# Attention in four 64x64 tiles, two sequences loaded head by head, and its vector and scalar work dealt out over the slots behind each burst

## The chip, the cores and the metric

The kernel runs on one core of one Trainium2 chip. The metric is the device time of one execution in microseconds (us), the median over several executions; lower is better. The profile is of one execution. Its span is some 1.8 us shorter than the device time of the same run (217.5 against 219.34 for the kernel before). The engines are TensorE (PE in the profile, and PEld for its weight loads), VectorE (DVE), ScalarE (ACT), GpSimd (POOL) and SyncE (SP). L and a number is the source line that issued an instruction, and the numbers differ from kernel to kernel.

## The reference

Retention with a decay per head, then a feed-forward layer with the snake activation. It is cut to what matters.

```python
# q, k, v: (4 sequences, 8 heads, 768 tokens, 64)
gamma = 1.0 - 2.0 ** (-5.0 - np.arange(H))
for t in range(S):
    state = gamma * state + outer(k[:, :, t], v[:, :, t])     # 64 x 64 per head
    y[:, :, t] = scale * einsum('bhd,bhde->bhe', q[:, :, t], state)
x = y.transpose(0, 2, 1, 3).reshape(3072, 512)
h = x @ w_in                                                  # 512 -> 2048
g = h + sin(alpha * h) ** 2 / (alpha + 1e-9)
out = g @ w_out                                               # 2048 -> 512
```

## The kernel before

The 768 tokens of a sequence are six chunks of 128. `order` puts the first chunks of the four sequences (e0 to e3) in front, then the others sequence by sequence; P[14] is the first of the others of sequence 2. The 24 chunks form groups of 4, 2, 4, 4, 4, 4 and 2 for the feed-forward layer (the MLP). In "phase g", TensorE alternates between slots of the first matmul of group g and pieces of the second matmul of group g - 1; the attention for group g + 1 is put between them in short bursts.

A burst has four parts: the scores q·k, the mixing of the masked scores with v, the part from earlier chunks (q times the state), and the sums k·v that go into the state.

```python
    def scale_v(j, eng):                       # decay of v inside a chunk
        eng.tensor_mul(raw["v", j], raw["v", j], kg[:, j % NCH, :, None].to_broadcast([128, H, D]))
    ...                                        # cut: GpSimd does it between the loads, early

    def stage_S(j):                            # sums: the state stays in PSUM for the whole sequence
        c = j % NCH
        if c == 0:
            st["ps"] = psum.tile([128, NP, D], F32, name="ps", tag="ps")
        ps = st["ps"]
        for p in range(NP):
            for e in range(2):
                nc.tensor.matmul(ps[64 * e:64 * e + 64, p, :], raw["k", j][:, 2 * p + e, :], raw["v", j][:, 2 * p + e, :],
                                 start=(c == 0 and p == 0), stop=True, skip_group_check=True)
        return ps

    def keep_S(j, ps):                         # ScalarE casts it straight from PSUM
        for e in range(2):
            r = slice(64 * e, 64 * e + 64)
            nc.scalar.copy(s_bd[(j % NCH + 1) % 2][r, :, r], ps[r, :, :])

    def stage_M(j):
        ...                                    # cut: inter and mixing matmuls into py (one bank, tag "ty")
        ps = stage_S(j) if c < NCH - 1 else None
        nc.vector.tensor_mul(x, py, qg[:, c])  # xT, the input of the MLP
        if ps is not None:
            keep_S(j, ps)

    def phase(g, outs, att, nf=1):
        no, done = len(outs), 0
        for n in range(FF // nf):
            now = Slot(g, n * nf, nf=nf).sq("A")   # first matmul, Sin and Square on ScalarE
            for fn in att.get(n, ()):
                fn()                               # attention of this slot, if any
            now.add()                              # VectorE: gT = h + sin^2 / alpha
            while done < no * (n + 1) * nf // FF:
                outs[done]()                       # a piece of the second matmul
                done += 1
```

PSUM has eight banks here: four rotating ones ("mm"), two for the scores ("pa"), one for py ("ty") and one for the state ("ps").

## Time and profile before

| | before |
|---|---|
| time, median (range) | 219.22 us (219.15 to 219.43) |
| span of the profiled run | 217.5 us, full clock |
| busy share: TensorE, ScalarE, VectorE, GpSimd | 94%, 75%, 59%, 41% |
| stores of the state for the next chunk | 40 ScalarE casts from PSUM, 0.36 us each |
| scalings of v | 21 on GpSimd (1.06 us each), 3 on VectorE (0.74 us) |

TensorE is busy nearly all the time, so an engine beside it may be idle or late without cost as long as TensorE never waits for it. The prediction below shows the lines that say so. The columns are start (us), duration (us), engine, source line, operation, output and inputs, shapes, count, and in brackets the wait ahead of it.

### The profile page before, as it was taken

Reading aid. Unit: us, or ns where it says so; the run is one execution under the profiler, and the core shown is the slowest. Engines: PE = TensorE matmul, PEld = TensorE weight load, DVE = VectorE, ACT = ScalarE, POOL = GpSimd, SP = SyncE. Lnnn points to the kernel's source line nnn. Section 1 sums busy time; section 2 is a strip of 40 time slices with the busy share of each in tenths; the row PEclk is TensorE's granted clock in tenths of the full one; section 3 lists DMA queues with packets and bytes.
Section 4 is the critical chain, followed back from the end, with each engine's and each line's share of the span. In section 5 each row is a group of like instructions: output and inputs, shape, how many; then the busy total and the mean of one; then the engine's idle time right before and its main releaser. Section 6 shows DMA issues by size and latency. Waiting matters only on the chain.

```text
span 217.5 us, 4218 instructions
## 1 busy us (share of the span) xinstructions
PE 203.8 (94%) x1634; PEld 107.5 (49%) x1661; DVE 128.1 (59%) x213; ACT 162.8 (75%) x311; POOL 90.1 (41%) x105
## 2 busy tenths in 40 slices
PE   7798899999989999999999999999999999999992
PEld 3444554467764545445455445454544544555540
DVE  4686659867895767766466566366464555233310
ACT  7678796658889999789768768777868876766610
POOL 8975335999889885896981000000000000000000
PEclk9999999999999999999999999999999999999999
DMA  9999999999999999999999146237011101111121
GB/s 132 151 193 191 205 207 164 154 207 161 164 151 182 163 120 154 112 160 175 135 188 107 23 96 77 60 60 96 7 47 51 48 0 51 48 48 48 51 94 50
DMA packets 99508, 24.67 MB, mean 113 GB/s; under 512 B 92304, under 2 KB 96416, under 8 KB 99488
## 3 DMA queue, kind: packets, MB, share of 16 engines
q0 software_dynamic: 77024, 13.37, 84.0%
q1 hardware_dynamic: 22464, 11.02, 26.4%
q8 instruction: 13, 0.21, 0.4%
q14 instruction: 7, 0.06, 0.1%
HBM read 27.27 MB, written 6.29 MB: 154 GB/s over the span
## 4 chain that ended last, share of the span: by engine, by line
PE 74%; DVE 9%; DMA 4%; POOL 4%; ACT 4%; issue 3%; POOLq 0%; ACTq 0%
PE po L304 35%; PE ph L279 31%; DMA qkr<-in_k_dram 4%; DVE gT L294 4%; PE py L247 3%; PE pa L213 2%; POOL qkr L83 2%; ACT s L282 2%; DVE aT L217 2%; PE py L251 2%; POOL vr L83 1%; DVE xT L258 1%; PE ps L227 1%; DVE s L289 1%; ACT s L287 1%
## 5 line engine op out<-in xcount | busy, mean ns | idle before, releaser
L294 DVE SCALAR_TENSOR_TENSOR gT<-s,rec_alpha,ph 128x512 bf16<-128x512 f32 (+3 forms) x120 | 74.1, 637 | 68.1 <-ACT s L287 67.5
L279 PE MATMUL ph<-xT,w_in 128*128 128x512 bf16 (+3 forms) x478 | 97.9, 336 | 1.1 <-DVE gT L294 0.6
L304 PE MATMUL po<-w_out,gT 128*128 128x512 bf16 x360 | 94.1, 379 | 3.8 <-issue 2.9
L282 ACT ACTIVATE s<-ph,alpha_sb 128x512 f32<-128x512 f32 (+3 forms) x120 | 69.6, 601 | 34.0 <-PE ph L279 33.9
L279 PEld LDWEIGHTS <-w_in 128*128 128x128 bf16 x480 | 45.5, 98 | 42.6 <-issue 2.1
L287 ACT ACTIVATE s<-s 128x512 f32<-128x512 f32 (+1 forms) x94 | 58.4, 621 | 2.6
L304 PEld LDWEIGHTS <-gT 128*128 128x128 bf16 x384 | 35.2, 98 | 38.2 <-issue 0.6
L112 POOL TENSOR_TENSOR vr<-vr,kg 128x512 bf16<-128x512 bf16 x21 | 22.0, 1056 | 12.2 <-DMA vr<-in_v_dram 12.2
L217 DVE TENSOR_TENSOR aT<-pa,mask 128x1024 bf16<-128x1024 f32 x20 | 24.4, 1220 | 0.3 <-PE pa L213 0.3
L83 POOL DMA_DIRECT2D vr<-in_v_dram x24 | 21.7, 904 | 3.0 <-DMA w_in<-in_moe_w_in_dram 1.7
L83 POOL DMA_DIRECT2D qkr<-in_q_dram x23 | 21.3, 925 | 4.0 <-DMA w_out<-in_moe_w_out_dram 1.6
L83 POOL DMA_DIRECT2D qkr<-in_k_dram x23 | 20.4, 887 | 3.8 <-DMA w_out<-in_moe_w_out_dram 3.3
L234 ACT CAST s_bd<-ps 64x256 bf16<-64x256 f32 x40 | 14.4, 360 | 2.4 <-PE ps L227 2.1
L316 ACT COPY o_sb<-po 128x512 f32<-128x512 f32 x23 | 13.1, 576 | 3.9 <-PE po L304 3.9
L258 DVE TENSOR_TENSOR xT<-py,qg 128x512 bf16<-128x512 f32 x20 | 13.7, 684 | 2.6 <-PE py L251 2.5
L328 PE MATMUL spare<-warm 128*128 128x512 bf16 x27 | 9.3, 465 | 1.4 <-DVE warm L131 1.2
L213 PEld LDWEIGHTS <-qkT 64*128 64x128 bf16 x192 | 5.4, 94 | 9.3 <-issue 7.1
L251 PE MATMUL py<-aT,vr 128*64 128x128 bf16 x192 | 9.5, 220 | 0.4 <-DVE rec_alpha L366 0.2
L213 PE MATMUL pa<-qkT 64*128 64x128 bf16 x192 | 9.5, 219 | 0.4 <-ACT qkT L186 0.2
L247 PE MATMUL py<-qkT,s_bd 128*64 128x128 bf16 x160 | 8.3, 224 | 0.7 <-DVE xT L258 0.7
L247 PEld LDWEIGHTS <-s_bd 128*64 128x64 bf16 x160 | 5.4, 109 | 4.8 <-issue 2.0
L251 PEld LDWEIGHTS <-vr 128*64 128x64 bf16 x192 | 6.9, 110 | 1.3 <-issue 1.0
(59 smaller groups left out, 68.8 us busy)
## 6 DMA issues: line engine op xcount, KB each, us to landing
out_dram<-o_sb SPq DMA_DIRECT2D x24, 256.0 KB, 2.3
vr<-in_v_dram POOLq DMA_DIRECT2D x24, 128.0 KB, 6.2
qkr<-in_q_dram POOLq DMA_DIRECT2D x23, 128.0 KB, 5.6
qkr<-in_k_dram POOLq DMA_DIRECT2D x23, 128.0 KB, 5.8
w_in<-in_moe_w_in_dram POOLq DMA_DIRECT2D x4, 512.0 KB, 11.1
w_out<-in_moe_w_out_dram POOLq DMA_DIRECT2D x4, 512.0 KB, 14.8
q<-in_q_dram SPq DMA_DIRECT2D x1, 256.0 KB, 3.4
k<-in_k_dram SPq DMA_DIRECT2D x1, 256.0 KB, 4.7
```

Of the source, the lines that this page charges most:

```text
L83: nc.gpsimd.dma_start(out=t, in_=chunk_of(src, j))
L112: eng.tensor_mul(raw["v", j], raw["v", j], kg[:, j % NCH, :, None].to_broadcast([128, H, D]))
L213: nc.tensor.matmul(pa[:, e, p, :], qkT[r, NP + p, :], qkT[r, p, :], start=(p == 0), stop=True, skip_group_check=True)
L217: nc.vector.tensor_mul(aT.rearrange("p e n t -> p (e n) t"), pa.rearrange("p e n t -> p (e n) t"), m)
L247: nc.tensor.matmul(py[r, p, :], s_bd[c % 2][:, p, r], qkT[:, p, :], start=(p == 0), stop=True, skip_group_check=True)
L251: nc.tensor.matmul(py[64 * e:64 * e + 64, p, :], vs[:, 2 * p + e, :], aT[:, e, p, :], start=(c == 0 and p == 0), stop=True, skip_group_che ...
L258: nc.vector.tensor_mul(x, py, qg[:, c])
L279: nc.tensor.matmul(self.ph[:, m, :], w_in[:, i, f * 128:(f + 1) * 128], xT[g][:, i, self.lo:self.hi], start=(m == 0 and i == 0), stop=(i = ...
L282: nc.scalar.activation(out=self.s[:, m, :], in_=self.ph[:, m, :], func=ACTF.Sin, scale=alpha_sb[:, f:f + 1])
L287: nc.scalar.activation(out=self.s, in_=self.s, func=ACTF.Square)
L294: nc.vector.scalar_tensor_tensor(gT[self.g][:, f, self.lo:self.hi], self.s[:, m, :], rec_alpha[:, f:f + 1], self.ph[:, m, :], op0=ALU.mult ...
L304: nc.tensor.matmul(po[g, ts], gT[g][:, f, ts * C:(ts + 1) * C], w_out[:, f, :], start=(f == 0), stop=(f == FF - 1))
```

## The change

The intent: use the array of TensorE as four independent 64x64 tiles, so that a burst becomes shorter; skip the triangle above the diagonal, for which two of the four sequences are loaded so that heads, not tokens, lie in the two halves of the partitions; and spread VectorE's and ScalarE's work behind a burst over the following slots, so that none of it holds up the MLP. To give four tiles separate banks, py becomes two banks, and the bank that held the state goes: the state is now kept in SBUF in float32, VectorE adds each chunk's sums to it, and ScalarE casts the result. The diff, cut to its core:

```diff
+    def wide(j):                                   # sequences 2 and 3, but for their first chunks
+        return j % NCH > 0 and j // NCH >= 2
+    def load_seq(bt):                              # one DMA per head and tensor, 640 rows each
+        ...
+        for i, src in enumerate((q, k, v)):
+            for h in range(H):
+                ...
+                nc.gpsimd.dma_start(out=o, in_=src[bt, h, C:, :].rearrange("(f i) d -> i f d", i=64))
...
+    def keep(j, py, base=256):
+        new = py[:, :, base:base + 128].rearrange("p b (m d) -> p m b d", m=2)
+        if j % NCH == 0:
+            nc.vector.tensor_copy(s_f, new)
+        else:
+            nc.vector.tensor_add(s_f, s_f, new)
+    def hand_on(j):
+        i = (j % NCH + 1) % 2
+        if not wide(j + 1):
+            nc.scalar.copy(s_n[i], s_f)
+            return
+        s = s_w[i].rearrange("p m b (y d) -> p m (b y) d", y=2)
+        nc.scalar.copy(s[half(0), :, 0:4:3], s_f[half(0)])
+        nc.scalar.copy(s[half(1), :, 1:3], s_f[half(1)])
...
+        def leave():
+            if now is not None:
+                keep(now, py)
+            nc.vector.tensor_mul(x_of(j), py[:, :, 0:256]..., qg[:, c]...)
+        return [leave, lambda: now is not None and hand_on(now)]
+
+    def burst(old, new, first=None):
+        inter(old)
+        return scores(new) + mix(old, first)       # [mask, leave, hand_on], dealt out later
...
-            now = Slot(g, n * nf, nf=nf).sq("A")
+            now = Slot(g, n * nf, nf=nf)
+            if rest and rest[0][0] == "A":
+                rest.pop(0)[1]()                   # hand_on, between Sin and Square
+            now.sq("A")
             for fn in att.get(n, ()):
-                fn()
+                more = fn()
+                if more:
+                    rest.extend(zip("DDA" if len(more) == 3 else "DA" if len(more) == 2 else "D", more))
...
             now.add()
+            if calm and rest and rest[0][0] == "D":
+                rest.pop(0)[1]()                   # one piece per slot (in phase 1 all at once)
...
+            at(a - 3, V(j))                        # scaling of v by VectorE, three slots ahead of its burst
```

Besides, the last tile of the output is computed and stored in pieces of 256, 128 and 128 columns. Also cut here: the chunk P[6] is transposed by a DMA and no longer by TensorE, a piece of w_in comes in three DMAs instead of one, and the scores of the next chunk now stand inside a burst, between its part from earlier chunks and its mixing.

## The prediction

> **What bounds the kernel now.** I read the page's shares and chain first, to see which engine sets the end; then busy time by stage, to see where other engines come near it; then the timeline of TensorE around one attention burst, which is what the change rebuilds; last GpSimd's timeline, because the order of the loads changes.
>
> ```profile
> PE 203.8 (94%) x1634; PEld 107.5 (49%) x1661; DVE 128.1 (59%) x213; ACT 162.8 (75%) x311; POOL 90.1 (41%) x105
> ...
> PE 74%; DVE 9%; DMA 4%; POOL 4%; ACT 4%; issue 3%; POOLq 0%; ACTq 0%
> ```
>
> TensorE is the bound, with 94% of the span and 74% of the chain. The rest of the chain lies almost wholly before 65 us.
>
> Busy time of each engine by stage; I cut at the phases of the MLP (start and group 0; phase 1 from 48.2; phases 2, 3, 4, 5, 6 from 65.1, 91.1, 123.6, 155.8, 185.7; then the tail). Columns: stretch, length, PE, PEld, DVE, ACT, POOL with counts, clock, DMA share, GB/s.
>
> ```profile
> 48.20:65.10 16.90, 15.64 (x222) 12.03 (x225) 14.06 (x25) 14.40 (x33) 15.42 (x18) 1.00 2.00 161
> 65.10:91.10 26.00, 25.11 (x214) 12.49 (x217) 18.49 (x25) 22.83 (x41) 21.07 (x23) 1.00 1.94 149
> 91.10:123.60 32.50, 31.87 (x262) 15.82 (x264) 18.67 (x24) 26.06 (x48) 20.71 (x23) 1.00 1.62 136
> ```
>
> In the steady phases (3 on) TensorE is full and nothing else is close. A 512-column matmul takes 0.216 us of pitch (four in 0.86 us in the chain), so phase 3 is 128 x 0.216 = 27.6 us of MLP, and the other 4.9 us are attention. In phase 1 and 2 VectorE (14.1 of 16.9) and ScalarE (22.8 of 26.0) stand nearer. The DMA engines hold about two packets each at any moment until 123 us.
>
> One burst of phase 3 on TensorE, in the timeline:
>
> ```profile
> 101.22 0.40 PE L213 MATMUL pa<-qkT 64*128 64x128 bf16 x8
> 101.55 0.41 PE L247 MATMUL py<-qkT,s_bd 128*64 128x128 bf16 x8
> 101.79 0.39 PE L251 MATMUL py<-aT,vr 128*64 128x128 bf16 x8
> 102.02 0.29 PE L227 MATMUL ps<-vr,qkr 128*64 128x64 bf16 x8
> ```
>
> Eight 128-column matmuls occupy 0.40 us from first start to last end and one lasts 0.22, so the eight starts spread over 0.18 us: three steps of some 58 ns, two matmuls to a step. Half-array tiles already run in pairs. The 64-column sums step by about 31 ns per pair (0.29 - 0.196 over three steps). From 101.22 to 101.55 are 0.33 us for four steps of 58: the remaining 0.1 us is the change of tile shape. The same 0.1 us separates a burst from the MLP on both sides. So a burst costs 0.1 + 0.23 + 0.1 + 0.25 + 0.22 + 0.12 + 0.1 = 1.12 us; the scores alone 0.43, the mixing alone 0.79.
>
> GpSimd's timeline, the loads of the last chunk of sequence 1 and the first of sequence 2:
>
> ```profile
> 63.14 0.94 POOL L83 DMA_DIRECT2D qkr<-in_q_dram  x1
> 64.07 0.88 POOL L83 DMA_DIRECT2D qkr<-in_k_dram  x1
> 64.94 0.90 POOL L83 DMA_DIRECT2D vr<-in_v_dram  x1
> 65.83 2.07 POOL L112 TENSOR_TENSOR vr<-vr,kg 128x512 bf16<-128x512 bf16 x2
> 67.82 0.94 POOL L83 DMA_DIRECT2D qkr<-in_q_dram  x1
> ```
>
> An issue of 1024 rows costs GpSimd 0.88 to 0.94 us, and a chunk with its scaling about 4 us; the page gives 0.79 for a weight load of 512 rows.
>
> **What the Trainium skill says.** "TensorEngine Tiling (Array Packing)", section Key Properties: tiles run independently, and changing the tiling mode drains the engine. The trace agrees: pairs in 58 ns, 0.1 us at each change. "TensorE: Matmul & The Clock Gate", section The mechanism (Part 3): matmuls on disjoint row and column tiles overlap, their starts some 4 ns apart. Pairs here are 4 ns apart; four at once is not shown by this trace. "VectorE: DVE Perf Modes", section Side-by-side: about 150 cycles of fixed cost, and in the plain mode, which PSUM operands leave, one element per cycle at 0.96 GHz. For the 1024-wide mask (1024 + 150)/0.96 = 1223 ns; the trace has 1220.
>
> **The change part by part.**
>
> *Bursts, sequences 2 and 3 (head by head).* Inter: 4 full-array matmuls of 128 columns, 4 x 56 = 0.22, and no change of shape ahead of it. Change 0.1. Scores: per m one group of four 128-column and one of four 64-column tiles, 2 x (56 + 31) = 0.17, as the triangle above the diagonal is left out. Mix the same, 0.17. Sums: four groups of four, 4 x 31 = 0.12. Change 0.1, plus 0.04 for the first four weight loads. Sum 0.93 us against 1.12. *Bursts of sequences 0 and 1:* change 0.1, inter 2 x 56, scores 4 x 56, change 0.1, mix 0.22, sums 0.12, change 0.1: 0.97.
>
> Before, each phase also paid separately for the first scores and the last mix. From the phases: attention before is 4.6 (phase 2), 4.9, 4.6 and 2.2 (phase 5) = 16.2 us. After: phase 2 has three bursts of 0.97 and a mixed one of about 0.92, 3.85; its first scores (0.42) move in front; phase 3 is 4 x 0.93; phase 4 the same plus 0.1 for sums of another shape; phase 5 is 0.93 + 0.6. Sum 13.3. Gain 2.9 us, all on the path, as TensorE is the bound there. Phases 0 and 1, counted the same way with one transposition by TensorE fewer (0.45): 9.1 to 8.0, gain 1.1.
>
> *VectorE.* Each chunk gains an addition of the state, 256 wide, (256 + 150)/0.96 = 0.42 us. The wide mask falls from 1.22 to (768 + 150)/0.96 = 0.96. Fourteen scalings of v, 0.74 each, come from GpSimd (two are those of e2 and e3). Phase 2 then holds 16 x 0.745 of gT, four bursts at about 2.3, six scalings and, at its head, the new masks, two clears and the mask of the first scores (about 3): 28 us of VectorE for some 24.6 of TensorE. Most of that is backlog which three free PSUM banks can carry; I charge 0.5. Phase 1 adds 0.42 per burst where TensorE already waits 0.7 us for xT in all (the list of waits): +0.6. The shared two-bank py must be evicted before the first burst: +0.6.
>
> *Start.* Three issues per w_in piece instead of one delay the loads behind by some 2.5 us of issuing, but those land after a DMA backlog of over 9 us (the chain's longest DMA step, 9.44), so hidden. The transposition of e3 goes one slot later and fills most of its 1.2 us stall: -0.7. New tables (about 1.1 us of small VectorE work) sit ahead of the mask of e2, which releases the last xT before the MLP: +0.7.
>
> *Tail.* Now: last eviction 0.42 on VectorE, then 0.37 on ScalarE, then a 256 KB store. After: 128 columns, 0.29 us, and a quarter of the bytes: -0.8.
>
> *The loads of sequence 2.* Two thirds of it, q and k of all heads (16 issues), must land before chunk P[14] can be transposed; before, one chunk was enough. P[13] reuses the buffer of e1, free after the burst of slot 6 in phase 1, near 61.5 us. P[13] takes 2.7, the 16 issues of 640 rows about 0.8 each, 12.8, and landing 5.7 (the page): about 82. The transposing DMA takes 6.0 (its median): 88. The burst that needs it is in slot 13 of phase 2: 65 + 13 x 1.29 + three bursts and slack of 0.5 = 85.2. A stall of about 2.8 us.
>
> Sum: -2.9 - 1.1 + 0.5 + 0.6 + 0.6 + 0 - 0.8 + 2.8 = -0.3 us. I don't take it whole. The slots of the transpositions and scalings are set so finely, and only two sequences are loaded this way, that the author probably saw this wait and placed the burst behind it; I halve the stall and take a quarter off the three charges of 1.7: -0.3 - 1.4 - 0.4 = -2.1, 217.1 us.
>
> **Rivals.** (1) No load stall: loads run ahead since GpSimd no longer waits for v (12.2 us of waits on the page). For it: rows per DMA shrink from 1024 to 640. Against it: issuing, not data, then sets the pace. Time 219.2 - 3.1 = 216.1, and 214.4 if the three charges of 1.7 fall away too. (2) Load stall in full or worse, with transposes slower under it (longest landing 8.9 us), and the clock dropping in the gap: 219 to 222. (3) The four tiles don't run at once, weights loading in pairs: the 64-column groups take 62 instead of 31, +0.25 per wide burst, ten bursts, so 217.1 + 2.5 = 219.6. Half-array pairs at 31 ns speak against it. (4) VectorE bounds phase 2 wholly: +3 us, but this hides the load stall, as both delay the same slots: 218.6.
>
> **Range and chances.** All four tiles, no stall and no charge give 214.4; the stall with a cold clock 220 to 221. Range 214.2 to 220.4. Faster by over 2% means under 214.9, which needs nearly every gain and no stall: 0.17. Slower by over 2% means above 223.6: 0.04. Within 2%: 0.79.
>
> **What will show it.** Wide bursts of 0.93 us between MLP matmuls (if 1.2, the tiles don't overlap). Phase 3 of 31.4 us instead of 32.5. In phase 2 a wait of TensorE on the transposed qkT of P[14], near 85 us. VectorE above 90% busy in phase 2. The end 2.8 us or less after the last eviction. The prediction is wrong if phase 3 doesn't shorten, or if a wait outside phase 2 exceeds 2 us.

## More of the kernel before

One more piece of that timeline is needed for the comparison: what happens after a burst of phase 3.

```profile
101.32 0.69 ACT L282 ACTIVATE s<-ph,alpha_sb 128x512 f32<-128x512 f32 x1 [0.38 <-PE ph L279]
...
102.05 0.63 ACT L287 ACTIVATE s<-s 128x512 f32<-128x512 f32 x1
...
102.47 0.81 PE L304 MATMUL po<-w_out,gT 128*128 128x512 bf16 x3 [0.16 <-issue]
102.58 0.73 ACT L234 CAST s_bd<-ps 64x256 bf16<-64x256 f32 x2
102.80 0.68 DVE L258 TENSOR_TENSOR xT<-py,qg 128x512 bf16<-128x512 f32 x1
```

ScalarE finishes the slot's Sin and Square first, and then casts the state, which waits for nobody but TensorE. VectorE has only the mask and the product xT to do.

## The result, and the profile after

The changed kernel takes 233.13 us (232.25 to 233.76, four runs) against 219.19 us of the kernel before in the same rounds. The ratio is 1.0635, 95% interval 1.0595 to 1.0676: 6.35% slower. The profiled run was at full clock. A ratio here is the mean time of one kernel's fast runs over that of the other's in the same rounds, so it is not quite the ratio of the medians that are quoted. Executions over 1.5% slower than the fastest of the same kernel are left out of the means.

The page's shares and chain of the changed kernel:

```profile
PE 202.1 (87%) x1921; PEld 108.3 (47%) x1949; DVE 144.1 (62%) x261; ACT 160.4 (69%) x301; POOL 86.0 (37%) x115
...
PE 48%; ACT 21%; DVE 14%; issue 9%; DMA 6%; SPq 0%; DVEq 0%; ACTq 0%
```

TensorE's busy time is even a little less than before, and no other engine is near being full. But TensorE's share of the chain that ended last fell from 74% to 48%, and ScalarE and VectorE came in with 21% and 14%. Nothing new is a bound; TensorE waits more. Busy time in the changed kernel's phases 2, 3 and 4 (the columns are as in the prediction):

```profile
72.30:103.10 30.80, 24.38 (x250) 12.03 (x254) 23.76 (x37) 21.50 (x37) 26.59 (x38) 1.00 2.06 159
103.10:136.30 33.20, 31.35 (x333) 15.65 (x337) 21.56 (x32) 25.51 (x45) 3.86 (x6) 1.00 0.60 84
136.30:170.50 34.20, 31.65 (x324) 15.75 (x328) 22.16 (x33) 25.44 (x45) 0.00 (x0) 1.00 0.30 63
```

Phase 2 takes 30.8 us instead of 26.0 and phase 3 33.2 instead of 32.5, with up to 6.4 us of TensorE idle in phase 2 against 0.9 (26.00 - 25.11) before; a few matmul records are missing in both. VectorE is busy for 77% of phase 2 (23.76 of 30.80), so it doesn't bound that phase. (Phase 1 is another matter: see e11.)

Are the bursts shorter? One burst of phase 3 on TensorE, in the timeline (the weight-load lines inside the burst are left out):

```profile
122.12 0.39 PE L347 MATMUL py<-qkT,s_w 128*128 128x128 bf16 x4
...
122.43 0.25 PE L372 MATMUL pa<-qkT 64*64 64x128 bf16 x4
...
122.51 0.20 PE L376 MATMUL pa<-qkT 64*64 64x64 bf16 x4
...
122.63 0.23 PE L394 MATMUL py<-aT,v_seq 64*64 64x128 bf16 x4
...
122.80 0.30 PE L313 MATMUL py<-v_seq,qk_seq 64*64 64x64 bf16 x16
123.03 0.55 PEld L463 LDWEIGHTS <-gT 128*128 128x128 bf16 x4
```

Yes. From the first inter matmul to the first MLP weights after the burst are 0.91 us. (The trace lacks the record of that first MLP matmul. In the complete trace of e3_both, below, the gap between MLP matmuls is 0.917 us.) The prediction's 0.93 and the four overlapping tiles hold. The time is lost beside the bursts, and the list of waits names where:

```profile
ACT s_n L328 <- DVE s_f L322: 6.3, 6, 2.2
...
PEld L390 <- DVE vr L142: 4.4, 4, 2.0
PEld L352 <- ACT s_n L328: 4.2, 4, 1.5
...
PE py L390 <- DVE vr L142: 3.5, 3, 1.9
...
PE ph L439 <- DVE xT L406: 3.3, 4, 1.4
...
PE ph L439 <- ACT o_sb L467: 2.5, 8, 1.0
```

Each line is the waiting engine, what it waited for, us in all, times, and the longest. Of these the list of the kernel before has only TensorE's waits for the cast state (1.3 us) and for an eviction (0.2 us). Now ScalarE waits 6.3 us for VectorE's addition of the state, TensorE waits for the cast state (s_n), for scaled v (vr), for the product xT and for ScalarE's eviction of an output tile (o_sb). Two of these are worth reading closely. First, what follows a burst of phase 3, in the timeline:

```profile
126.70 0.69 ACT L442 ACTIVATE s<-ph,alpha_sb 128x512 f32<-128x512 f32 x1 [0.38 <-PE ph L439]
127.02 0.41 DVE L322 TENSOR_TENSOR s_f<-s_f,py 128x256 f32<-128x256 f32 x1
...
127.47 0.40 ACT L331 CAST s_w<-s_f 64x256 bf16<-64x256 f32 x1
127.88 0.40 ACT L332 CAST s_w<-s_f 64x256 bf16<-64x256 f32 x1
...
128.31 0.63 ACT L447 ACTIVATE s<-s 128x512 f32<-128x512 f32 x1
128.85 0.57 ACT L467 COPY o_sb<-po 128x512 f32<-128x512 f32 x1
...
129.46 1.02 PE L439 MATMUL ph<-xT,w_in 128*128 128x512 bf16 x4 [0.21 <-ACT o_sb L467]
```

ScalarE does the same two casts as before, but now between the slot's Sin (L442) and its Square (L447). The Square comes 0.8 us later, the eviction behind it as well, and TensorE stands for 0.375 us, because it needs the PSUM bank that this eviction frees. (From the first of the four matmuls before it, at 128.22, to 129.46 are 1.24 us, and four take 0.86; the 0.21 in the bracket counts from the modelled end of the fourth.) This happens seven times in phases 3 to 5, 2.6 us in all. Second, the burst of slot 13 of phase 2, of which the prediction expected a wait for the transposed P[14]:

```profile
89.16 3.68 SPq L262 DMA_TRANSPOSE qkT<-qk_seq  x2
...
95.81 0.23 PE L372 MATMUL pa<-qkT 64*64 64x128 bf16 x4
...
96.03 0.69 DVE L142 TENSOR_TENSOR vr<-vr,kg 128x512 bf16<-128x512 bf16 x1
...
97.28 0.69 DVE L142 TENSOR_TENSOR vr<-vr,kg 128x512 bf16<-128x512 bf16 x1
...
98.02 0.41 PE L390 MATMUL py<-aT,vr 128*64 128x128 bf16 x8 [1.87 <-DVE vr L142]
```

The scores of P[14] start at 95.81 with no wait for qkT. It is close, though: the transposition was issued at 89.16 and took 5.92 us to land (the profile keeps the landing of each DMA), so it landed at 95.08. The same burst waits 1.87 us for something else: VectorE's scaling of v, which stands in its row behind other pieces.

To see in which half the time goes, I take one landmark that all kernels share, the start of ScalarE's eviction of the seventh output tile (the first one stored in phase 3), read from each trace:

| kernel | start to 7th tile | 7th tile to end of span | of this, 7th to 11th tile (one phase) |
|---|---|---|---|
| before | 99.1 | 118.4 | 32.24 |
| changed | 112.4 | 118.6 | 34.24 |

So 13.3 us are lost in the start and phases 0 to 2, and in the second half the shorter bursts and the shorter tail are just eaten up (+0.2 us).

### The profile page after: what moved, and what is told of

Its sections match the earlier page's. It is cut to its first block, busy times and chain, and to the rows that moved or that the text cites. A ratio compares the mean times of both kernels' runs of the same rounds, so it can differ in the third digit from the quotient of the medians.

```text
span 231.0 us, 4807 instructions
## 1 busy us (share of the span) xinstructions
PE 202.1 (87%) x1921; PEld 108.3 (47%) x1949; DVE 144.1 (62%) x261; ACT 160.4 (69%) x301; POOL 86.0 (37%) x115
## 4 chain that ended last, share of the span: by engine, by line
PE 48%; ACT 21%; DVE 14%; issue 9%; DMA 6%; SPq 0%; DVEq 0%; ACTq 0%
PE ph L439 20%; PE po L463 18%; ACT s L447 9%; ACT s L442 7%; DVE gT L454 5%; DMA qkT<-qkr 4%; DVE s_f L322 2%; ACT o_sb L467 2%; DMA o_sb<-in_k_dram 2%; PE poh L478 2%; ACT s_w L332 1%; DVE xT L406 1%; DVE vr L142 1%; DVE aT L279 1%; PE py L390 1%
## 5 line engine op out<-in xcount | busy, mean ns | idle before, releaser
L442 ACT ACTIVATE s<-ph,alpha_sb 128x512 f32<-128x512 f32 (+3 forms) x120 | 69.5, 600 | 43.9 <-PE ph L439 42.9
L447 ACT ACTIVATE s<-s 128x512 f32<-128x512 f32 (+1 forms) x94 | 58.4, 621 | 2.3
L104 POOL DMA_DIRECT2D qk_seq<-in_q_dram x16 | 11.6, 776 | 6.8 <-DMA qkr<-in_q_dram 2.8
L367 DVE TENSOR_TENSOR aT<-pa,mask 128x1024 bf16<-128x1024 f32 x10 | 12.1, 1214 | 3.1 <-PE pa L363 3.1
L89 POOL DMA_DIRECT2D vr<-in_v_dram x14 | 12.7, 909 | 1.2 <-DMA w_out<-in_moe_w_out_dram 1.0
L104 POOL DMA_DIRECT2D qk_seq<-in_k_dram x16 | 11.6, 742 | 3.9 <-DMA qk_seq<-in_q_dram 3.7
L89 POOL DMA_DIRECT2D qkr<-in_q_dram x13 | 12.0, 921 | 1.6 <-DMA w_out<-in_moe_w_out_dram 1.1
L89 POOL DMA_DIRECT2D qkr<-in_k_dram x13 | 11.7, 900 | 2.2 <-DMA w_out<-in_moe_w_out_dram 1.7
L104 POOL DMA_DIRECT2D v_seq<-in_v_dram x16 | 11.4, 758 | 0.3 <-DMA qk_seq<-in_k_dram 0.3
L381 DVE TENSOR_TENSOR aT<-pa,maskq 128x768 bf16<-128x768 f32 x10 | 9.5, 951 | 0.0
L322 DVE TENSOR_TENSOR s_f<-s_f,py 128x256 f32<-128x256 f32 x16 | 6.6, 415 | 1.0 <-PE py L310 1.0
L142 DVE TENSOR_TENSOR v_seq<-v_seq,kgq 128x512 bf16<-128x512 bf16 x10 | 6.8, 684 | 0.0
```

Of the source, the lines that this page charges most:

```text
L89: nc.gpsimd.dma_start(out=t, in_=chunk_of(src, j))
L104: nc.gpsimd.dma_start(out=o, in_=src[bt, h, C:, :].rearrange("(f i) d -> i f d", i=64))
L322: nc.vector.tensor_add(s_f, s_f, new)
L367: return [lambda: nc.vector.tensor_mul(aT.rearrange("p e n t -> p (e n) t"), pa.rearrange("p e n t -> p (e n) t"), mask_bc)]
L381: return [lambda: nc.vector.tensor_mul(aT, pa[:, :, 0:384].rearrange("p e (m t) -> p e m t", m=2), maskq[:, None, None, :].to_broadcast([1 ...
L442: nc.scalar.activation(out=self.s[:, m, :], in_=self.ph[:, m, :], func=ACTF.Sin, scale=alpha_sb[:, f:f + 1])
```

## The experiments

Twelve kernels ran. "c" stands for the changed kernel. The theory after reading the trace: the tiles gain what was predicted; the time goes into hand-overs between the two in-order queues of VectorE and ScalarE. Rivals: the head-by-head loads cost it; or VectorE is simply too full, whatever the order.

### e1_cast_dve: c with the casts on VectorE

```diff
-            nc.scalar.copy(s_n[i], s_f)
+            nc.vector.tensor_copy(s_n[i], s_f)
...                                       # the two casts of s_w the same; hand_on is called at the end of leave()
-                    rest.extend(zip("DDA" if len(more) == 3 else "DA" if len(more) == 2 else "D", more))
+                    rest.extend(zip("DDD", more))
```

> Only the last step of the state's way is moved: the cast of the summed state to bf16 is done by VectorE straight after its own addition, not by ScalarE. Theory 1 (the state's way through two in-order queues is the main cost: ScalarE stands behind VectorE, squares and evictions stand behind ScalarE's casts): the 0.375 us stall of TensorE after each burst of phases 3 to 5 goes (ten of them, 3.7 us), the 2.4 us wait for the eviction near 43 us goes, phase 1 gains about 2: 225 to 228 us. Theory 2 (the scaling of v by VectorE just ahead of its use is the main cost): VectorE gets more work, so no gain, 232 to 236. Rival (late loads of sequences 2 and 3): no change, 233.

Measured: 228.07 us (227.21 to 228.67), ratio 1.039 (1.0339 to 1.0441), 5.1 us less than c and at the upper end of theory 1. The stalls of 0.375 us behind the bursts are gone in its trace (there were seven, not the ten of the expectation). The wait of ScalarE for VectorE's addition was real, and it was passed on to TensorE. The edit moves the cast to another engine and also to an earlier place, so it doesn't say which of the two counts.

### e2_scale_pool: c with v scaled by GpSimd again

```diff
-    load_seq(2)
-    load_seq(3)
+    scale_v(P[10], nc.gpsimd)
+    load_seq(2, {(0, 1): P[11], (0, 3): P[12], (0, 5): P[13], (0, 7): e2})    # after those loads
+    load_seq(3, {(0, 3): e3})
...
-            at(a - 3, V(j))
-            if new is not None and new % NCH == 1:
-                at(a - 4, V(new - 1))
+            if wide(j):
+                at(a - 3, V(j))
```

> Only the scaling of v of the four chunks of phase 2 and of e2 and e3 goes back to GpSimd, between the issues of the loads, where GpSimd waits for the DMA anyway; the scaling of the head-by-head chunks stays on VectorE. Theory 2: the waits of the mixing matmuls for vr (4.4 us on the weight loads) go and phase 2 loses its VectorE backlog: 226 to 229 us. Theory 1: only the part of phase 2, 229 to 232, with the 0.375 us stalls left as they are. Rival (late loads): the loads of sequence 2 come 2 to 4 us later still, 233 to 237.

Measured: 229.73 us (229.14 to 232.81), ratio 1.0459 (1.0417 to 1.0502), 3.4 us less than c. Its profiled run was the slow one of the four, so I read no durations from it.

### e3_both: e1 and e2 together

> Both edits at once. If theories 1 and 2 name separate costs the gains add: 219 to 224 us. If both relieve the same wait, the time is that of the better one alone. What is then left above 219 is neither, and late loads or the shared two-bank tile are next.

Measured: 224.08 us (223.8 to 230.14), ratio 1.0207 (1.0169 to 1.0245), 9.0 us less than c. The two gains add up (5.1 + 3.4 = 8.5): they are two different waits. Its trace, which is complete, shows a new one. VectorE and GpSimd in the timeline, the cast of a state and what GpSimd does meanwhile:

```profile
51.01 2.25 DVE L330 CAST s_n<-s_f 128x256 bf16<-128x256 f32 x1
51.03 2.07 POOL L144 TENSOR_TENSOR vr<-vr,kg 128x512 bf16<-128x512 bf16 x2
```

This cast from SBUF to SBUF takes 0.28 us when GpSimd is quiet. Here it takes 2.25 us, over two scalings by GpSimd. The Trainium skill, "SBUF — State Buffer", section Who interferes with whom, says that VectorE's copies and casts can take a port pair that it shares with GpSimd, as an exclusive lock, and that the later one waits fully. This trace agrees. ScalarE has ports of its own by that page, and its casts in c are 0.40 us throughout. So moving the cast cures one wait and brings a risk.

### e4_no_wide: c without head-by-head loads

```diff
-        return j % NCH > 0 and j // NCH >= 2
+        return False
...
-    load_seq(2)
-    load_seq(3)
+    for n in range(14, NJ):
+        load_chunk(P[n])
```

Every chunk also has its own buffers again, as before the change (`bufs=NJ` instead of 12 and 14; cut here).

> No sequence is loaded head by head: every chunk is loaded as before and uses the form of sequences 0 and 1 (bursts of 0.97 instead of 0.93 us, mask of 1024 columns instead of 768); the dealing out, the scaling on VectorE and the casts on ScalarE stay. Rival (late loads): 4 us or more faster, 226 to 229. Theories 1 and 2: the stalls stay, and ten bursts with longer masks cost a little more: 232 to 235 us.

Measured: 230.94 us (230.8 to 233.65), ratio 1.0553 (1.0481 to 1.0625), 2.2 us less than c, between the two expectations; the intervals of the two overlap. Its trace is of the longest run, 2.7 us above the median, with TensorE at half clock for 3.4 us twice. It explains a gain of this size without the loads. A burst in chunk form takes 1.02 us instead of 0.92, but its state needs one ScalarE cast instead of two, and the 0.375 us behind each burst vanishes. Seven of these are 2.6 us, against nine bursts that are 0.1 us longer. That leaves little for the loads, but this run doesn't settle how much: in the traced execution the scores of P[14], here a whole chunk, waited 1.97 us for their own transposition, which took 8.9 us. A wait of the kind that the prediction feared thus came without head-by-head loads.

### e5_state_first: e3 with another order behind each burst

```diff
             if now is not None:
                 keep(now, py)
+                hand_on(now)
             nc.vector.tensor_mul(x_of(j), ...)
-            if now is not None:
-                hand_on(now)
...
-        return scores(new) + mix(old, first)
+        mask = scores(new)
+        return mix(old, first) + mask
```

> On top of both edits (cast by VectorE, scaling by GpSimd): behind each burst the state's addition and cast and the product that gives xT come before the mask of the next scores, not after it. Theory 1 carried on (VectorE's order is the path: the next burst waits for the state, and the next phase waits for the last xT): the stalls at the phase boundaries (1.6, 0.7 and 0.7 us in the run with both edits) and most of 3 us of waits for the state in phase 1 go: 218.5 to 220.5 us from 224.1. Rival (VectorE's amount of work is the limit, not its order): no gain, 223 to 225.

Measured: 227.75 us (226.41 to 228.39), ratio 1.0369 (1.0332 to 1.0405): 3.7 us more than e3, a clear miss. In its trace the waits at the ends of phases 2 to 4 did shrink (from 1.59 to 0.33 us at the first). But in phase 1 and at the start of phase 2, bursts follow each other closely, and the next scores wait for the score bank that the late mask still holds (three waits of 3.0 us in all). Three gaps of 2.9 to 3.3 us there (bursts included) were followed by some 3 us in which matmuls started 0.43 us apart instead of 0.216, at half clock.

### e6_turn_early: e5 with the transposition of P[5] earlier, and both halves of the shared two-bank tile finished before either is evicted

```diff
-        if f == FF - 1:
-            o_sb = ...; nc.scalar.copy(o_sb, po[g, ts]); nc.sync.dma_start(...)
+        if f == FF - 1 and (g, ts) != (0, 0):
+            for t in ((0, 1) if (g, ts) == (0, 1) else (ts,)):
+                o_sb = ...; nc.scalar.copy(o_sb, po[g, t]); nc.sync.dma_start(...)
...
+    stage_T(P[5], nc.scalar)
     run(scores(P[4]))
     begin(e0)
```

> On top of that: the last matmuls of the shared two-bank accumulation are issued before its first half is evicted, and the transposition of P[5] goes some matmuls earlier, where ScalarE is free, so that its copy no longer stands ahead of the evictions. If the 1.4 us wait for the eviction near 43 us comes from these two: 1.2 to 1.6 us less than the run before, 217 to 219. If the shared banks hold the burst up anyway: within 0.4 us of it.

Measured: 227.0 us (226.09 to 228.23), ratio 1.0356 (1.0311 to 1.04), 0.75 us less than e5, between the two expectations. The intervals of the two overlap, so I count this as a hint at most.

### e7_clean_no_wide: e5 without head-by-head loads, all scaling on GpSimd

The edits of e4 on e5, with `scale_v(P[n - 2], nc.gpsimd)` between the loads.

> The version with the state first, but with no sequence loaded head by head, and all v scaled by GpSimd behind its load as before the change. Rival (the loads): 1.5 us or more faster than the version with the state first, as the first test without such loads was 2.2 us faster than the changed kernel. My theory: there the gain came through the scaling and the deadlines in phase 2, which are gone by now, so the longer bursts and masks decide: the same to 1 us slower, 219 to 221.

Measured: 226.71 us (226.44 to 227.29), ratio 1.0333 (1.0303 to 1.0362), 1.0 us less than e5, again between the two expectations. The intervals overlap, so that the head-by-head form, with its scaling by VectorE and its shorter bursts, costs anything here is a hint at most. It is not the cause of 14 us.

### e8_before_tail: the kernel before, with the last tile in pieces

```diff
-    for fn in out_pieces(NG - 1, range(sizes[-1])):
+    for fn in out_pieces(NG - 1, range(sizes[-1] - 1)):
         fn()
+    last_tile(NG - 1, sizes[-1] - 1)          # 256, 128 and 128 columns, as in c
```

> The kernel before with one part of the change alone, the last tile in three pieces of 256, 128 and 128 columns. From the traces the time from the last matmul to the end falls from 4.3 to 3.1 us: 1.0 to 1.2 us faster, 218.1 to 218.4. If the shorter matmuls pay for it, no change.

Measured: 218.28 us (217.68 to 219.75), ratio 0.9953 (0.9922 to 0.9985), 1.15 us less than before. The tail's gain is real. It is inside c as well.

### e9_hybrid: the tiles on the old arrangement

The kernel before in phases 0 to 2 for sequences 0 and 1 (state in PSUM, one ScalarE cast, scaling on GpSimd), with e8's tail. Only sequences 2 and 3 are loaded head by head and done in four tiles, with two separate one-bank tiles for py. The core of the edit:

```diff
+    def burst_q(old, new, first=None, last=False):
+        inter_q(old)
+        mask = scores_q(new)
+        state, leave = mix_q(old, first)
+        return leave + state + mask if last else state + mask + leave    # one piece per slot
```

> The tiles on the kernel before's own arrangement. Sequences 0 and 1 are done exactly as in the kernel before (loads of whole chunks, state accumulated in PSUM and cast once by ScalarE, scaling on GpSimd); only sequences 2 and 3 are loaded head by head and done in four 64x64 tiles, with two separate one-bank tiles instead of the shared two-bank tile, state addition and cast both on VectorE, and one piece of VectorE work per slot behind each burst; the last tile is stored in pieces as in e8_before_tail. Theory (the tiles gain what was predicted, the time is lost in the hand-over of work between engines): 219.4 - 2.9 (phases 3 to 6, attention 16.2 to 13.3 us) - 1.1 (tail) = 215.4 us, between 214.5 and 217.5, and the wide bursts take 0.93 us. Rival (the head-by-head loads and the 64x64 tiling cost as much as they gain): 218.3 or more, no better than e8_before_tail.

Measured: 228.37 us (224.9 to 230.42), but three of the six runs were slow. The fast ones took 224.9, 225.06 and 227.9, ratio 1.0298 (1.0242 to 1.0354): some 10 us off. I had made the mistake of the change once more. Its list of waits:

```profile
PEld L370 <- DVE xT L395: 7.8, 10, 1.3
...
PE py L370 <- DVE xT L395: 4.2, 5, 0.8
PEld L370 <- DVE s_w L325: 3.9, 1, 3.9
PE py L370 <- DVE s_w L325: 3.4, 1, 3.4
```

The product xT, which frees the banks of py, was third in the row, and bursts come every three slots; so five bursts took 2.42 us instead of 1.14 (the expectation of e12 below says seven, which is a miscount). One cast from SBUF (s_w) ran into GpSimd's scalings and issues and took 2.49 us for its two instructions, and that burst took 4.5 us; TensorE then ran at half clock for a while.

### e10_order_late: e3 with e5's order in phases 3 to 5 alone

```diff
             if now is not None:
                 keep(now, py)
+                if wide(j):
+                    hand_on(now)
...
-        return scores(new) + mix(old, first)
+        mask = scores(new)
+        return mix(old, first) + mask if wide(old) else mask + mix(old, first)
```

> e3_both with the order state, xT product, mask behind the bursts of phases 3 to 6 alone; in phases 0 to 2 the mask stays first, as in e3_both. If e5_state_first lost its 3.7 us in phases 0 to 2 alone (scores waiting for the bank that the late mask holds, then TensorE at half clock), while its shorter stalls in phases 3 to 5 were a true gain of 3 bursts x some 0.4 us a phase and 3 boundaries x 0.4 to 1.2 us, then this takes 220 to 222.5 us, 2 to 4 under e3_both. Rival (the late mask costs in every phase, or the gain is taken back elsewhere): 223.5 to 228 us.

Measured: 223.55 us (222.45 to 228.16, five runs), ratio 1.0167 (1.0134 to 1.02), 0.5 us less than e3; the intervals overlap. The expectation of 2 to 4 us missed, and the rival's number came out, at its edge. The expectation had counted three stalls per phase that e3 no longer had. What it settles: e5's loss came from phases 0 to 2, as e10 differs from it only there and takes 4.2 us less. Its profiled run was its slow one, so its trace isn't used.

### e11_state_direct: e10 with the state written straight from PSUM

```diff
-            nc.vector.tensor_copy(s_n[i], s_f)          # after the addition, from SBUF
+            nc.vector.tensor_add(s_n[i], s_f, new)      # before it, new in PSUM; for s_w the same by halves
...
-    later_mask()                                        # between phases 1 and 2
-    for t in s_w:
-        nc.vector.memset(t, 0.0)
+    at(2, lambda: [later_mask])                         # in slots of phase 2
+    at(6, lambda: [lambda: [nc.vector.memset(t, 0.0) for t in s_w]])
```

> e10_order_late with the state in bf16 written straight from PSUM by one addition in place of the cast of the finished sum from SBUF, and put first behind each burst of a whole chunk; the mask table and the clearing of the state tiles stand in phase 2 instead of at the end of phase 1. If the long casts (0.28 us normally, 1.2 to 2.25 us while GpSimd issues loads) and the place of the cast behind mask, addition and product make the stalls of phase 1 (waits for s_n of 2.4 us and, for the mask, 2.2 us), then these fall by 2 to 4 us: 219.5 to 221.5 us. Rival (VectorE is simply full in phase 1, whatever the order): 222.5 to 224 us, as e10_order_late.

Measured: 223.68 us (223.08 to 224.09), ratio 1.0187 (1.0161 to 1.0212): nothing gained over e10, so the rival's number came out. The direct addition takes a steady 0.41 us, and the long casts are gone, but phase 1 stalls as before. The timeline there shows why:

```profile
63.74 0.42 DVE L335 TENSOR_TENSOR s_n<-s_f,py 128x256 bf16<-128x256 f32 x1
...
64.08 1.22 DVE L377 TENSOR_TENSOR aT<-pa,mask 128x1024 bf16<-128x1024 f32 x1
...
65.22 0.68 DVE L417 TENSOR_TENSOR xT<-py,qg 128x512 bf16<-128x512 f32 x1
65.81 0.41 DVE L324 TENSOR_TENSOR s_f<-s_f,py 128x256 f32<-128x256 f32 x1
...
66.28 0.31 PE L362 MATMUL py<-qkT,s_n 64*64 64x128 bf16 x8 [1.17 <-DVE s_f L324]
```

The next burst may not write py before VectorE has done all four of these: state, mask, product and addition, about 2.5 us from 63.74 to 66.22, whatever their order. Before, the sums had a bank of their own, which ScalarE read, and only mask and product (1.9 us) were VectorE's. That the missing bank, not the order, is what binds phase 1 is argued from this chain; no run gave py a second pair of banks, as PSUM has none left.

Two rivals are untested, and the traces speak for both. The first is VectorE's amount of work, as the expectation had it: in e3 VectorE was busy for 17.58 of the 18.85 us of phase 1 (51.9 to 70.75), 93%, in e11 for 16.61 of 18.95 (53.4 to 72.35), 88%, and before for 14.06 of 16.90. The second is the transposing DMAs. The first four that phase 1 issues took 5.5 to 7.6 us to land in the kernel before, and 8.1 to 10.0 in the changed one. Where the state came sooner, TensorE ran into them, as in e3, in the burst that corresponds to the one above:

```profile
65.03 0.42 PE L365 MATMUL pa<-qkT 64*64 64x128 bf16 x16 [0.25 <-DMA qkT<-qkr]
```

In e11 this transposition landed at 66.24, 0.04 us before the burst began. With a free bank the scores would still have waited for it, so the bank alone can't be worth the 1.17 us there.

### e12_hybrid_two: e9 with its waits mended

```diff
+                    nc.vector.tensor_add(o, s_f[half(e), :, b, :], n)     # bf16 state straight from PSUM
...
-        return leave + state + mask if last else state + mask + leave
+        both = leave + state if last else state + leave
+        return [lambda: [f() for f in both]] + mask                       # state and xT one piece, mask the second
...                                                                        # first state of sequence 2 one slot earlier
```

> e9_hybrid with its two waits mended. In its trace seven wide bursts took 2.42 us instead of 1.14, because they waited for the xT product of the burst before, which frees the two banks of py and stood third in the row of one piece per slot; one burst took 4.5 us, waiting for the first state of sequence 2, whose cast from SBUF to SBUF took 2.49 us instead of 0.58 while GpSimd issued loads; TensorE then ran some 3 us at half clock. Here state and xT product are one piece, the mask the second; the state in bf16 is added straight from PSUM instead of cast from SBUF; the first state of sequence 2 is begun one slot earlier. Theory (the tiles are worth 2.9 us and the tail 1.1 where no burst has to wait): 228.4 - 7 x 1.28 - 3.4 - 1.2 = 214.8 us, between 214 and 217.5. Rival (the longer VectorE work of a slot takes a part back, or the loads cost): 218.3 or more.

Measured: 217.47 us (216.0 to 219.29), ratio 0.9886 (0.9854 to 0.9918), the fastest of all; its interval just doesn't meet that of e8 (0.9922 to 0.9985). It lies at the edge of what was expected; with five bursts instead of seven, the sum of the expectation gives 217.4 instead of 214.8. The bursts that took 2.42 us are back at 1.14 (a missing record of 0.216 us included in both). I had expected the whole 2.9 us of the prediction, but part of that belonged to phase 2, which this kernel leaves as it was. Against e8, each compared with the kernel before in its own rounds, it is 0.0067 of 219.5, or 1.5 us.

The landmarks once more, with the mended kernels (spans of profiled runs; e12's was its slowest run, 1.8 us above its median):

| kernel | start to 7th tile | 7th tile to end | 7th to 11th tile |
|---|---|---|---|
| before | 99.1 | 118.4 | 32.24 |
| changed | 112.4 | 118.6 | 34.24 |
| e3_both | 106.1 | 115.9 | 32.19 |
| e11_state_direct | 107.3 | 114.5 | 31.46 |
| e8_before_tail | 98.7 | 117.4 | 32.24 |
| e9_hybrid | 98.6 | 127.1 | 41.11 |
| e12_hybrid_two | 102.0 | 115.5 | 31.99 |

The 102.0 of e12 holds 3.4 us at half clock (from 21 to 24.4 us). e9, whose phases 0 to 2 are nearly the same, ran at full clock up to its seventh tile and reached it at 98.6, like e8: the old arrangement of these phases loses nothing, although sequences 2 and 3 are loaded head by head in it.

## Why the prediction was wrong, point by point

**Bursts: right.** 0.93 us predicted for the head-by-head form, 0.92 measured. For bursts in chunk form it said 0.97, and 1.02 was measured in the complete traces. One sum behind the gain is off: attention in phase 2 before was 26.0 - 96 x 0.216 = 5.3 us by the subtraction that gave the other phases, not 4.6.

**The gain of the later phases: right, but only once the waits were mended.** By the prediction's own figures, phases 3 to 5 and the tail together should gain 11.7 - 9.1 + 0.8 = 3.4 us. In e11, from the seventh tile to the end, they gain 118.4 - 114.5 = 3.9. In the changed kernel they lose 0.2. Phase 3 became 2.0 us longer by the landmark (0.7 by the cut at the phases; the landmark's stretch reaches into phase 4, whose first burst waits for VectorE's scaling), where 1.1 shorter was predicted, and e11's is 0.8 shorter. The prediction had named this as what would prove it wrong, and also a wait over 2 us outside phase 2: TensorE waits 2.6 us near 43 us, in phase 0, for ScalarE's eviction of one half of the shared tile, and ScalarE before that 2.28 us for VectorE's copy of the first state.

**The failed step: the VectorE charges, "+0.5", "+0.6" and "+0.6", and the sentence that most of it "is backlog which three free PSUM banks can carry".** They added up VectorE's busy time and asked whether it fits. In phase 2 it fits: VectorE worked 23.76 us there (77%), where 28 us and over 90% were predicted. What costs is where each piece stands in its queue and who waits for it. The hand-over of the state had been one step, a pair of ScalarE casts from PSUM; it became a chain of VectorE and ScalarE, and the prediction gave it no charge beyond the addition. The Trainium skill, "TensorE: Matmul & The Clock Gate", section Architectural detail: the array is 16× 32×32, not 1× 128×128, calls ScalarE's and VectorE's queues strict FIFO; the traces agree: the Square shown above started at 128.31, behind the two casts, though its Sin had ended at 127.39. By the runs, in place of the charges of 1.7 us stand:

- 5.1 us for ScalarE's casts of a state that VectorE adds (e1);
- 3.4 us for VectorE's scaling of v shortly before its use (e2), for which the prediction charged only busy time, inside the +0.5;
- about 8 us before the seventh tile that remain in e11 (107.3 against 99.1), most of it in phases 0 and 1. Here the prediction had expected a gain of 1.1. The shared py and the longer VectorE round fit the waits seen in phase 1, but so do VectorE's amount of work and the slower transposing DMAs there (see e11); how much of the 8 us belongs to each, to e6's half tile and to the loads was not measured apart, and this part of the cause stays open. That the old arrangement of these phases, with the scores of P[14] moved to phase 3, avoids all of it is shown by e9 (98.6).

**"A stall of about 2.8 us" for the loads: did not occur, by luck.** The loads were later than predicted, not earlier: the last of q and k landed at 86.4 us (predicted: about 82) and the transposition at 95.08 (predicted: 88). TensorE reached this burst only at 95.7 instead of 85.2, because it had waited elsewhere. In e3 and e11 the transposition landed just 0.14 and 0.21 us before the scores began, so by these landings a kernel without the other waits would have met this stall. e9 and e12 avoid it by taking these scores in phase 3. That the same burst stalled for 1.87 us by another cause would have made the prediction look confirmed if only the burst, and not the releaser, had been read.

**Start "-0.7 + 0.7": can't be told.** The first MLP matmul starts 0.6 us later (16.07 against 15.49 us), but runs with the same start differ as much: e8, whose start is that of the kernel before, has 15.96, and e1, whose start is the changed kernel's, 15.18.

**Tail "-0.8": right, a little small.** From the last matmul's end to the end are 3.0 us instead of 4.1, and e8 gained 1.15.

**The final adjustment was the wrong way.** The prediction halved the stall and took a quarter off the charges, on the ground that the author had probably seen such waits. That is a guess about a person, and no view of the profile stood behind it. Rival 4, VectorE as the bound of phase 2, came nearest in place and was still wrong in kind: in phase 2 VectorE didn't bound, it was late.

## What to carry to other kernels

When a change moves work between engines, don't only add busy time; draw for each hand-over the row in which the piece will stand, what is ahead of it, and which bank is held until it is done. An operation that reads PSUM and waits for TensorE alone is worth keeping as it is, even on a busier engine; splitting it into two engines' queues cost more here (5 us) than the tiles gained (some 3). A burst shortened by 0.2 us pays only if everything that frees its banks ends before the next burst.

## What the Trainium skill lacked or had wrong

- "TensorEngine Tiling (Array Packing)", Key Properties, says that a change of tiling mode drains the engine, but gives no size. Here a change of shape costs about 0.1 us: from 122.12 to 122.43 are 0.31 us, and the four 128-column matmuls between step by 0.056.
- The same page doesn't say by what step one group of four tiles follows another. Here a group of four 64-column tiles steps by about 0.03 us, and one of four 128-column tiles by 0.06 to 0.08.
- "SBUF — State Buffer" has the lock between VectorE and GpSimd right. In its section Who interferes with whom it mentions a measurement of VectorE 6.8 times slower; here a short cast beside a run of scalings became 8 times slower, 2.25 us instead of 0.28 (e3), and two casts took 2.49 us instead of 0.58 (e9).
- "TensorE: Matmul & The Clock Gate", section HAM oscillation — how this bites in real kernels, warns of idle gaps over some 3.4 us. Here 3.42 us without a matmul (e9, 99.06 to 102.48) were followed by half clock, in agreement. But shorter stretches were enough elsewhere: two of 1.94 us, 2.6 us apart, in e5 and one of 1.97 us in e4. One of 2.44 us was followed by half clock in e4 (43.73 to 46.16) and not in the changed kernel (43.48 to 45.92).
